# Gated linear recurrence and ELU layer on one core: one activation table set for Ln and Exp, and a remade opening list

## The chip, the cores and the metric

The kernel runs on one core of a Trainium2 chip. The metric is the time of one execution on the device in microseconds, the median of several runs. The core has five engines with queues of their own, each in program order: TensorE (PE, with its weight loads, PEld), VectorE (DVE), ScalarE (ACT), GpSimd (POOL) and SyncE (SP), which here only issues transfers. They wait for each other by semaphores.

## The reference

```python
mag = np.sqrt(a_re * a_re + a_im * a_im)
scale = np.minimum(mag, 0.999) / (mag + 1e-06)
a_re_n, a_im_n = (a_re * scale, a_im * scale)
for t in range(S):
    ar, ai = (a_re_n[:, :, t, :, None], a_im_n[:, :, t, :, None])
    new_re = ar * S_re - ai * S_im
    new_im = ar * S_im + ai * S_re
    kv = np.einsum('bhd,bhe->bhde', k[:, :, t], v[:, :, t])
    S_re, S_im = (new_re + kv, new_im)
    y[:, :, t] = np.einsum('bhd,bhde->bhe', q[:, :, t], S_re)
x = y.transpose(0, 2, 1, 3).reshape(B * S, H * D)
h = x @ w_in
g = np.where(h > 0.0, h, np.exp(np.minimum(h, 0.0)) - 1.0)
out = g @ w_out
```

B = 4 sequences, H = 8 heads, S = 768 steps, D = 48; x is 3072 x 384, w_in 384 x 2048, w_out 2048 x 384. The weights come as float64, all else as float32.

## The kernel before

**Units.** The work is cut into 12 units (u = 0 to 11) of 128 time steps of two sequences. For each unit the recurrence is turned into products: the decays' logarithms and angles are summed over time by matmuls with triangular constants, q and k are scaled by what comes out, and scores, states and outputs are matmuls. Then follows the two-layer part on the unit's 256 tokens.

**Steps of one unit that the change touches.** `squares` (L709, L710; in unit 0 `squared`, L705, by halves) and `joined` (L716, in unit 0 the matmuls of L720) make the squared magnitude. `logarithms` (L735, L736; unit 0: L731) takes Ln, `powers` (L746, L747; unit 0: L742) Exp of multiples of it, `lengths` (L772; unit 0: L766) and `ratios` (L757, L759, L760) and `slopes` (L780) combine these on VectorE. `angles` (L815; unit 0: L811) is an arctan, `carried` (L826) adds the last unit's turn to it. `decays` sums the lengths on TensorE (L889; L932 in unit 1; `sums` L872 and `summed` L879 in unit 0) and takes Exp of the sums (L904, L920). `turned` (L837 on TensorE, L842 to L849 on VectorE) sums the angles to z, `waves` (L973 to L977) takes sine and cosine of z. `scaled` (L982, L986, L992) and `gated` (L1003) put them on q and k; `transposed` (L1023, L1024), `scores` (L1031, L1036; `scored` L1136, L1145), `states` (L1064, L1077 to L1081) and `values` (L1100, L1109, copies L1121 to L1126; later L1177, L1180) follow, and `seam` (L1190) moves the last heads' rows by DMA. `noted` (L791; later L796, L799) checks that the inputs lie in the range in which this way is exact, by the constant `LEAST_RE`; were they not, a slower general path would run after it. `ends` takes the decay at the end of each half (L946 to L954).

**The two layers.** For units 0 to 2 `inner` (L1210) makes two blocks of 128 hidden columns in one PSUM tile `mlp`, of which there are three; `elu` (L1219, L1220 on ScalarE, L1221 on VectorE) empties it; `project` (L1235) multiplies by w_out in four parts of four blocks, with sums in the banks y0 and y1 or, for unit 0, in two of the `mlp` tiles. From unit 3 on (first layer) and unit 2 on (second layer) the products are done with fewer multiplications: `mult` (L1455), `product` (L1319) and sums on VectorE (`summed_in` L1403, L1405; `combined` L1278; `folded` L1297; L1471, L1480).

**Weights.** `fetch` loads a part (L644) as float64; there are eight parts of w_in and eight of w_out. Each call of `convert` puts one of the five VectorE instructions of a part's rounding to float32 in place (L40, L43, L46, L50, L655), so that they lie between other work. `warm` (L1557) is a filler: matmuls of the identity.

**What sets the order.** The scheduler is off (`manual_schedule`). The order in which the functions are called is the order on every engine: first the list `first`, written out by hand, for the opening (to about unit 3), and then a plan in which every step has a place by number (`put`), 16 places to a unit. A step that is in the list is left out of the plan. `table` (L1200) asks for an activation table set at its place; where the set in force lacks a function, a load is put before that function by itself, and is seen under its line.

Of the kernel before, what the change touches and what calls it, by code (L numbers as in the profile page):

```python
# [17 lines left out]
L = 64  # L18
CAP = 0.999
EPS = 1e-6  # L20
LEAST_RE = 0.7
MAGIC = 1.5 * 2.0**23
TURN = 6.2831850

# [481 lines left out]
def kernel(  # L506
# [12 lines left out]
    nc = tc.nc  # L519
# [489 lines left out]
    PAIRED = 2  # L1009
# [496 lines left out]
    def pronounced():  # L1506
# [6 lines left out]


    load_a(0)
    nc.scalar.preload_act_table_set("natural_log")
    ident = const(C, C, "ident")
    nc.gpsimd.memset(ident, 0.0)
    nc.gpsimd.affine_select(
        out=ident, in_=ident, pattern=[[-1, C]], base=0, channel_multiplier=1,  # L1520
# [57 lines left out]
    def gates_of(u, *at):  # L1578
# [5 lines left out]
    first = [  # L1584
        (warm, 1), (warm, 12), (fetch, "in", 0), (begun, 0), (inverses, 0), (inverses, 1),
        (load_qk, 0), (squared, "ar", 0), (load_v, 0), (squared, "ar", 1), (squared, "ai", 0),
        (joined, 0, 0), (squared, "ai", 1), (joined, 0, 1), (logarithms, 0, 0), (logarithms, 0, 1),
        (fetch, "in", 1), (fetch, "in", 2), (ratios, 0, 0), (lengths, 0, 0), (warm, 2), (warm, 1),
        (lengths, 0, 1), (sums, 1), *2 * [(convert,)], (table, "exp_and_others"), (ratios, 0, 1),
        (powers, 0, 0), (powers, 0, 1), (warm, 2), (sums, 0), (warm, 1), (angles, 0, 0),  # L1590
        (angles, 0, 1), (summed, 0), (summed, 1), (decayed, 0, 0), (turned, 0, 0), (decayed, 0, 1),
        (turned, 0, 1), (waves, 0, 0), (waves, 0, 1), (begun, 1), (scaled, 0, "q", 0), (warm, 1),
        (scaled, 0, "k", 1), (scaled, 0, "k", 0), (ends, 0), (scaled, 0, "q", 1), (warm, 1),
        (noted, 0), (convert,), (gated, 0, 0), (warm, 1), (warm, 2), (gated, 0, 1), (warm, 2),
        (convert,), (transposed, 0, "q", 0), (convert,), (transposed, 0, "k", 0),
        (table, "natural_log"), (carry_on, 0), (transposed, 0, "q", 1), (scores, 0, 0),
        *3 * [(convert,)], (load_a, 1), (transposed, 0, "k", 1), (states, 0, 0), (scores, 0, 1),
        (squares, 1), (joined, 1), (fetch, "in", 3), (convert,), (values, 0, 0), (logarithms, 1),
        (powers, 1), (convert,), (states, 0, 1), (warm, 2), (load_qk, 1), (convert,), (lengths, 1),
        (values, 0, 1), (ratios, 1), (seam, 0), (warm, 2), (decays, 1), (load_a, 2), (warm, 1),  # L1600
        (slopes, 1), (convert,), (angles, 1), (convert,), (noted, 1), (convert,), (ends, 1),
        (load_v, 1), (convert,), (turns, 1), (scaled, 1), (inner, 0, 0), (convert,), (inner, 0, 2),
        (fetch, "in", 4), (table, "trig_and_small", 1), (warm, 4), (waves, 1), (gated, 1, 0),
        (convert,), (elu, 0, 0), (convert,), (transposed, 1, "q", 0), (gated, 1, 1),
        (transposed, 1, "k", 0), (load_v, 2), (convert,), (inner, 0, 4), (convert,),
        (fetch, "in", 5), (scores, 1, 0), (states, 1, 0), *2 * [(convert,)],
        (transposed, 1, "k", 1), (convert,), (transposed, 1, "q", 1), (fetch, "in", 6),
        (inner, 0, 6), *2 * [(convert,)], (elu, 0, 2), (convert,), (fetch, "in", 7), (scores, 1, 1),
        (convert,), (values, 1, 0), (states, 1, 1), (values, 1, 1), *3 * [(convert,)], (warm, 2),
        (elu, 0, 4), (seam, 1), (convert,), (inner, 0, 8), *2 * [(convert,)], (inner, 0, 10),  # L1610
        (elu, 0, 8), (convert,), (fetch, "out", 0), (elu, 0, 6), (convert,), (inner, 1, 0),
        (elu, 0, 10), (convert,), (inner, 1, 2), *3 * [(convert,)], (fetch, "out", 1),
        (inner, 1, 4), (fetch, "out", 2), (inner, 0, 12), (fetch, "out", 3), (convert,),
        (inner, 0, 14), (elu, 1, 2), *3 * [(convert,)], (elu, 1, 4), (fetch, "out", 4), (convert,),
        (elu, 1, 0), (convert,), (elu, 0, 12), *2 * [(convert,)], (inner, 1, 6), (convert,),
        (fetch, "out", 5), *2 * [(convert,)], (elu, 0, 14), *3 * [(convert,)], (elu, 1, 6),
        (convert,), (begun, 2), (squares, 2), (convert,), (joined, 2), (convert,), (inner, 1, 8),
        (inner, 1, 10), (convert,), (inner, 1, 12), (fetch, "out", 6), (fetch, "out", 7),
        *2 * [(convert,)], (elu, 1, 8), (convert,), (elu, 1, 10), (convert,), (load_qk, 2),
        *3 * [(convert,)], (elu, 1, 12), *4 * [(convert,)], (project, 1, 0, 0, 4),  # L1620
        (project, 1, 1, 0, 4), (inner, 1, 14), (project, 0, 0, 0, 4), (logarithms, 2), (convert,),
        (powers, 2), (elu, 1, 14), (convert,), (ratios, 2), *2 * [(convert,)], (slopes, 2),
        (convert,), (lengths, 2), (noted, 2), *2 * [(convert,)], (load_a, 3), (angles, 2),
        (carried, 2), (project, 0, 1, 0, 4), (convert,), (project, 0, 0, 4, 8), (convert,),
        (project, 1, 0, 4, 8), *2 * [(convert,)], (project, 1, 1, 4, 8), (decays, 2),
        (table, "trig_and_small", 2), *3 * [(convert,)], (project, 1, 0, 8, 12), *2 * [(convert,)],
        (turns, 2), (project, 0, 1, 4, 8), (begun, 3), *2 * [(convert,)], (waves, 2), (squares, 3),
        (scaled, 2), (ends, 2), (gated, 2), (joined, 3), (project, 1, 1, 8, 12),
        (project, 1, 1, 12, 16), (logarithms, 3), (powers, 3), (states, 2, 0), (load_qk, 3),
        (project, 1, 0, 12, 16), (lengths, 3), (ratios, 3), (project, 0, 0, 8, 12),  # L1630
        (transposed, 2, "k", 0), (transposed, 2, "q", 1), (slopes, 3), (transposed, 2, "q", 0),
        (transposed, 2, "k", 1), (table, "trig_and_small", 3), (angles, 3), (scored, 2), (opened,),
        (carried, 3), (project, 0, 1, 8, 12), (valued, 2), (seam, 2), (noted, 3),
        (project, 0, 0, 12, 16), (summed_in, 0), (summed_in, 1), (combined, 1, 1), (turns, 3),
        (combined, 1, 0), (combined, 2, 0), (waves, 3), (summed_in, 2), (combined, 4, 0),
        (combined, 2, 1), (scaled, 3), (combined, 4, 1), (ends, 3), (load_v, 3), (load_a, 4),
        (project, 0, 1, 12, 16), (gated, 3, None, ('q',)), (inner, 2, 0), (elu, 2, 0),
        (gated, 3, None, ('k',)), (inner, 2, 2), (elu, 2, 2), (inner, 2, 4), (elu, 2, 4),
        (transposed, 3, "q", 0), (summed_in, 3), (inner, 2, 6), (elu, 2, 6), (folded, 2, 0, (3, 1)),
# [135 lines left out]
```

## Time and profile before

| what | us |
|---|---|
| median of three runs (667.33 to 667.91) | 667.35 |
| the profiled execution, its own time | 665.7 |
| its span, first to last instruction | 663.7 |
| PE busy, share of the span | 640.6, 97% |
| VectorE busy, share | 501.9, 76% |
| ScalarE busy, share | 418.9, 63% |
| period of a unit in the middle (L735 at 298.58, 348.92, 399.27) | 50.35 |
| first `inner` matmul of the long run in the opening | 72.21 |
| end of that run, first `project` | 101.23 |

Share of the span means time in which the engine executes an instruction, and in a row of a timeline the first number is the start in us from the span's start and the second the time from the first start to the last end of the instructions that it merges. What stands in square brackets is idle time before it and what ended that. PEclk is the granted share of TensorE's clock; it was 0.99 on average. The program sends 53.58 MB through its main queue, and in the first 25 us the transfers run at 170 GB/s.

### The profile page before, as it was taken

The page shows a single profiled execution, that of the slowest core. Times are in us where ns is not written, and L with a number is a line of the kernel's source. Part 1 is how long each engine was busy: PE and PEld are TensorE (multiplying, and loading weights), DVE is VectorE, ACT ScalarE, POOL GpSimd, SP SyncE. Part 2 cuts the span into 40 slices and gives each one's busy share as a digit, 9 for nine tenths or more (in the row PEclk, how much of TensorE's full clock was granted, in tenths as well). Part 3 has the DMA queues.
Part 4 walks back from the last instruction along what each step waited for, and adds up shares of the span by engine and source line. Part 5 has one row for each costly group of instructions (what it writes and reads, how often), then busy time and mean ns, then how long its engine had stood idle before and what let it go on. Part 6 is the DMA issues. An engine that isn't in the chain of part 4 may idle for free.

```text
span 663.7 us, 17229 instructions
## 1 busy us (share of the span) xinstructions
PE 640.6 (97%) x7236; PEld 580.2 (87%) x7236; DVE 501.9 (76%) x801; ACT 418.9 (63%) x684; POOL 153.8 (23%) x200
## 2 busy tenths in 40 slices
PE   8889999999999899999999999999999999999995
PEld 6868886576897898998998998998998999999995
DVE  5798999967868689578678678678668768764481
ACT  6885367586756566767667667667677677571250
POOL 2000000112124313413403503503503502402000
PEclk9799999999999999999999999999999999999999
DMA  9997745732800713333442442451451551212100
GB/s 164 178 146 117 150 143 155 131 74 48 128 2 16 136 35 85 80 84 80 77 93 72 78 99 62 83 106 50 93 105 46 100 105 44 53 33 61 35 2 30
DMA packets 151443, 56.12 MB, mean 85 GB/s; under 512 B 129684, under 2 KB 143164, under 8 KB 151356
## 3 DMA queue, kind: packets, MB, share of 16 engines
q1 hardware_dynamic: 147616, 53.58, 39.8%
q0 software_dynamic: 3520, 1.20, 1.6%
q8 instruction: 59, 0.97, 0.6%
q14 instruction: 28, 0.23, 0.1%
q10 hardware_dynamic: 220, 0.14, 0.1%
HBM read 48.91 MB, written 4.80 MB: 81 GB/s over the span
## 4 chain that ended last, share of the span: by engine, by line
PE 63%; DVE 14%; ACT 10%; issue 5%; DMA 4%; SPq 3%; DVEq 0%; ACTq 0%
PE mlp L1319 20%; PE mlp L1455 10%; PE mlp L1210 7%; PE y L1455 5%; PE w L1023 4%; DVE g L1471 4%; PE mlp L1235 3%; PE y L1235 3%; PE y L1109 3%; DVE g L1480 3%; SPq L598 3%; DMA w<-in_moe_w_in_dram 3%; PE w L1064 2%; PE w L837 2%; ACT ee L1477 2%
## 5 line engine op out<-in xcount | busy, mean ns | idle before, releaser
L1319 PE MATMUL mlp<-w_out,g 128*128 128x192 f32 x640 | 111.8, 328 | 1.0 <-DVE ee L1331 1.0
L1319 PEld LDWEIGHTS mlp<-w_out,g 128*128 128x128 f32 x640 | 104.2, 190 | 4.4 <-DVE ee L1331 1.6
L1081 POOL TENSOR_TENSOR S<-S,T 128x384 f32<-128x384 f32 x36 | 30.2, 839 | 174.0 <-DVE S L1079 174.0
L1210 PE MATMUL mlp<-x,w_in 128*128 128x256 f32 x288 | 65.1, 384 | 0.2
L1210 PEld LDWEIGHTS mlp<-x,w_in 128*128 128x128 f32 x288 | 54.7, 193 | 9.2 <-DVE g L1221 0.7
L1471 DVE TENSOR_TENSOR g<-g,mlp 128x512 f32<-128x512 f32 x45 | 30.6, 681 | 40.1 <-ACT qt L1024 28.6
L1297 DVE TENSOR_TENSOR g<-g 128x512 f32<-128x512 f32 x80 | 54.4, 694 | 5.0 <-PE mlp L1319 3.8
L1455 PE MATMUL mlp<-x,w_in 128*128 128x128 f32 x424 | 56.2, 275 | 0.4 <-DVE o L1344 0.4
L1480 DVE SCALAR_TENSOR_TENSOR g<-ee,g 128x512 f32<-128x512 f32 x63 | 47.5, 754 | 11.1 <-ACT ee L1477 11.0
L1319 PE MATMUL mlp<-w,g 128*128 128x192 f32 x320 | 54.5, 329 | 0.0
L1319 PEld LDWEIGHTS mlp<-w,g 128*128 128x128 f32 x320 | 51.8, 190 | 0.6
L1455 PEld LDWEIGHTS mlp<-x,w_in 128*128 128x128 f32 x424 | 51.6, 192 | 0.7 <-DVE o L1344 0.6
L1190 POOL DMA_DIRECT2D x<-y x62 | 29.9, 489 | 94.8 <-ACT y L1126 43.5
L1476 ACT ACTIVATE ee<-g 128x512 f32<-128x512 f32 x63 | 39.5, 627 | 17.4 <-DVE g L1471 17.0
L1468 ACT COPY g<-mlp 128x512 f32<-128x512 f32 x36 | 21.1, 585 | 43.9 <-PE mlp L1455 43.7
L1477 ACT ACTIVATE ee<-ee 128x512 f32<-128x512 f32 x72 | 45.4, 631 | 2.3
L1024 ACT COPY qt<-w 128x512 f32<-128x512 f32 x48 | 25.8, 591 | 15.6 <-PE w L1023 15.4
L904 ACT ACTIVATE n<-w 64x384 f32<-64x384 f32 (+1 forms) x60 | 28.1, 486 | 8.9 <-PE w L889 8.3
L973 ACT ACTIVATE cs<-n 128x768 f32<-128x768 f32 (+1 forms) x14 | 10.5, 751 | 35.7 <-DVE n L845 35.6
L1455 PE MATMUL mlp<-x,g 128*128 128x128 f32 x224 | 29.7, 275 | 1.2 <-DVE o L1344 1.2
L1079 DVE TENSOR_TENSOR S<-w,S 128x384 f32<-128x384 f32 x38 | 21.0, 553 | 12.2 <-POOL S L1081 10.0
L1455 PE MATMUL y<-x,w_in 128*128 128x128 f32 x216 | 29.0, 277 | 1.2 <-ACT g L1468 1.2
(222 smaller groups left out, 1428.7 us busy)
## 6 DMA issues: line engine op xcount, KB each, us to landing
w<-in_moe_w_out_dram SPq DMA_DIRECT2D x8, 768.0 KB
g<-in_moe_w_in_dram SPq DMA_DIRECT2D x24, 256.0 KB
g<-in_moe_w_out_dram SPq DMA_DIRECT2D x24, 256.0 KB
w<-in_moe_w_in_dram SPq DMA_DIRECT2D x16, 288.0 KB
vn<-in_v_dram SPq DMA_DIRECT2D x24, 192.0 KB
ar<-in_a_re_dram SPq DMA_DIRECT2D x22, 192.0 KB
ai<-in_a_im_dram SPq DMA_DIRECT2D x22, 192.0 KB
q<-in_q_dram SPq DMA_DIRECT2D x22, 192.0 KB
```

The source lines that it names most:

```text
L904: nc.scalar.activation(out=flat(x[key][to, n : n + 1]), in_=t[of], func=AF.Exp, scale=sign)
L1081: eng.tensor_tensor(out=new_s, in0=new_s, in1=wide, op=ALU.mult)
L1190: eng.dma_start(out=x["x"][ds(j * HP + D, G), i], in_=x["y"][ds(j * HP + i * G, G)])
L1210: nc.tensor.matmul(t[:, e], lhsT=w_in[:, i, ts(f + e, C)], rhs=x["x"][:, i], start=(i == 0), stop=(i == NI - 1),)
L1235: nc.tensor.matmul(x["o", n], lhsT=x["g", f // 8][:, f % 8, ts(n, C)], rhs=w_out[:, f], start=(f == 0), stop=(f == NF - 1),)
L1297: nc.vector.tensor_tensor(out=S_of(u, k, h), in0=a, in1=b, op=op)
L1319: nc.tensor.matmul(to, lhsT=a[:, m], rhs=b[:, m], start=(first and h == 0 and m == 0), stop=False, skip_group_check=True,)
L1455: nc.tensor.matmul(x["c" + c][:, ts(m, C)], lhsT=a[:, m], rhs=x["mix"][p], start=(p == BANKS[c][0] and m == 0), stop=False, skip_group_che ...
L1471: nc.vector.tensor_tensor(out=part(u, to), in0=part(u, a), in1=part(u, b), op=op)
L1476: nc.scalar.activation(out=e, in_=part(u, of), func=AF.Relu, scale=-1.0)
L1477: nc.scalar.activation(out=e, in_=e, func=AF.Exp, scale=-1.0)
L1480: nc.vector.scalar_tensor_tensor(out=part(u, to), in0=nat[u]["e", to], scalar=-1.0, in1=part(u, of), op0=ALU.add, op1=ALU.max,)
```

## The change

Four things are changed. The set `natural_log_exp_and_others` takes the place of `natural_log` and of `exp_and_others` wherever the kernel asks for a set. `LEAST_RE` is 0.7072. In unit 0 the half 0's Exp follows its Ln at once, and the decays stand ahead of the angles. And the list `first` is remade throughout: the order of unit 0 and unit 1, the places of loads and of fillers (37 in both, in other places), of the conversions, and of the steps of units 2 and 3; its end reaches a few steps further. The plan for later units keeps its places. The start of the list, to the first `elu`, its middle, and the rest of the diff:

```diff
-LEAST_RE = 0.7
+LEAST_RE = 0.7072
...
-    nc.scalar.preload_act_table_set("natural_log")
+    nc.scalar.preload_act_table_set("natural_log_exp_and_others")
...
-        (joined, 0, 0), (squared, "ai", 1), (joined, 0, 1), (logarithms, 0, 0), (logarithms, 0, 1),
-        (fetch, "in", 1), (fetch, "in", 2), (ratios, 0, 0), (lengths, 0, 0), (warm, 2), (warm, 1),
-        (lengths, 0, 1), (sums, 1), *2 * [(convert,)], (table, "exp_and_others"), (ratios, 0, 1),
-        (powers, 0, 0), (powers, 0, 1), (warm, 2), (sums, 0), (warm, 1), (angles, 0, 0),
-        (angles, 0, 1), (summed, 0), (summed, 1), (decayed, 0, 0), (turned, 0, 0), (decayed, 0, 1),
-        (turned, 0, 1), (waves, 0, 0), (waves, 0, 1), (begun, 1), (scaled, 0, "q", 0), (warm, 1),
-        (scaled, 0, "k", 1), (scaled, 0, "k", 0), (ends, 0), (scaled, 0, "q", 1), (warm, 1),
-        (noted, 0), (convert,), (gated, 0, 0), (warm, 1), (warm, 2), (gated, 0, 1), (warm, 2),
-        (convert,), (transposed, 0, "q", 0), (convert,), (transposed, 0, "k", 0),
-        (table, "natural_log"), (carry_on, 0), (transposed, 0, "q", 1), (scores, 0, 0),
-        *3 * [(convert,)], (load_a, 1), (transposed, 0, "k", 1), (states, 0, 0), (scores, 0, 1),
-        (squares, 1), (joined, 1), (fetch, "in", 3), (convert,), (values, 0, 0), (logarithms, 1),
-        (powers, 1), (convert,), (states, 0, 1), (warm, 2), (load_qk, 1), (convert,), (lengths, 1),
-        (values, 0, 1), (ratios, 1), (seam, 0), (warm, 2), (decays, 1), (load_a, 2), (warm, 1),
-        (slopes, 1), (convert,), (angles, 1), (convert,), (noted, 1), (convert,), (ends, 1),
-        (load_v, 1), (convert,), (turns, 1), (scaled, 1), (inner, 0, 0), (convert,), (inner, 0, 2),
-        (fetch, "in", 4), (table, "trig_and_small", 1), (warm, 4), (waves, 1), (gated, 1, 0),
-        (convert,), (elu, 0, 0), (convert,), (transposed, 1, "q", 0), (gated, 1, 1),
-        (transposed, 1, "k", 0), (load_v, 2), (convert,), (inner, 0, 4), (convert,),
-        (fetch, "in", 5), (scores, 1, 0), (states, 1, 0), *2 * [(convert,)],
-        (transposed, 1, "k", 1), (convert,), (transposed, 1, "q", 1), (fetch, "in", 6),
-        (inner, 0, 6), *2 * [(convert,)], (elu, 0, 2), (convert,), (fetch, "in", 7), (scores, 1, 1),
...
+        (squared, "ai", 1), (joined, 0, 0), (joined, 0, 1), (logarithms, 0, 0), (lengths, 0, 0),
+        (powers, 0, 0), (logarithms, 0, 1), (ratios, 0, 0), (sums, 0), (lengths, 0, 1), (sums, 1),
+        (warm, 2), (ratios, 0, 1), *2 * [(convert,)], (table, "trig_and_small", 0), (load_a, 1),
+        (fetch, "in", 1), (fetch, "in", 2), (angles, 0, 0), (turned, 0, 0), (angles, 0, 1),
+        (turned, 0, 1), (summed, 0), (powers, 0, 1), (decayed, 0, 0), (warm, 1), (summed, 1),
+        (decayed, 0, 1), (convert,), (waves, 0, 0), (waves, 0, 1), (scaled, 0, "k", 0),
+        (scaled, 0, "q", 0), (begun, 1), (table, "natural_log_exp_and_others", 0),
+        (scaled, 0, "k", 1), (scaled, 0, "q", 1), (ends, 0), (warm, 2), (warm, 1), (warm, 1),
+        (gated, 0, 0), (transposed, 0, "q", 0), (warm, 1), (squares, 1), (warm, 1), (gated, 0, 1),
+        (convert,), (transposed, 0, "k", 0), (noted, 0), (convert,), (joined, 1), (states, 0, 0),
+        (scores, 0, 0), *3 * [(convert,)], (load_qk, 1), (transposed, 0, "k", 1), (convert,),
+        (logarithms, 1), (powers, 1), (fetch, "in", 3), (lengths, 1), (states, 0, 1),
+        (transposed, 0, "q", 1), (values, 0, 0), (warm, 2), (ratios, 1), (scores, 0, 1), (convert,),
+        (noted, 1), (decays, 1), (values, 0, 1), (warm, 2), (seam, 0), (slopes, 1), (carry_on, 0),
+        *3 * [(convert,)], (ends, 1), (warm, 2), (warm, 2), (table, "trig_and_small", 1),
+        (convert,), (angles, 1), (warm, 1), (load_v, 1), (scaled, 1), (turns, 1), (waves, 1),
+        (inner, 0, 2), (inner, 0, 0), (fetch, "in", 4), (fetch, "in", 5), (load_a, 2),
+        (table, "natural_log_exp_and_others", 1), (gated, 1, 0), (gated, 1, 1), (convert,),
+        (elu, 0, 2), *2 * [(convert,)], (transposed, 1, "k", 0), (convert,),
+        (transposed, 1, "q", 0), *2 * [(convert,)], (transposed, 1, "q", 1), (scores, 1, 0),
+        (convert,), (states, 1, 0), (inner, 0, 4), *4 * [(convert,)], (transposed, 1, "k", 1),
+        (values, 1, 0), (scores, 1, 1), (fetch, "in", 6), (fetch, "in", 7), (states, 1, 1),
+        (warm, 4), (convert,), (elu, 0, 0), *2 * [(convert,)], (elu, 0, 4), (values, 1, 1),
+        (seam, 1), *2 * [(convert,)], (inner, 0, 8), (inner, 0, 6), (convert,), (elu, 0, 8),
+        *2 * [(convert,)], (inner, 1, 6), (inner, 1, 0), (fetch, "out", 0), (convert,),
...
+        *2 * [(convert,)], (elu, 0, 12), (convert,), (elu, 1, 10), *3 * [(convert,)], (load_qk, 2),
+        (convert,), (fetch, "out", 6), (convert,), (project, 1, 0, 0, 4), (convert,),
+        (inner, 1, 14), (slopes, 2), *4 * [(convert,)], (project, 1, 1, 0, 4),
+        (project, 0, 0, 0, 4), (angles, 2), (lengths, 2), (fetch, "out", 7), (convert,),
+        (project, 0, 0, 4, 8), (elu, 1, 14), (project, 0, 1, 0, 4), (decays, 2), *2 * [(convert,)],
+        (project, 1, 0, 4, 8), (carried, 2), (convert,), (table, "trig_and_small", 2), (convert,),
+        (turns, 2), (scaled, 2), (convert,), (table, "natural_log_exp_and_others", 2),
+        (project, 0, 1, 4, 8), (convert,), (begun, 3), (waves, 2), *2 * [(convert,)],
+        (table, "trig_and_small", 3), (project, 0, 1, 8, 12), (project, 1, 1, 4, 8), (squares, 3),
+        (gated, 2), (project, 1, 0, 8, 12), *2 * [(convert,)], (joined, 3), (convert,),
+        (transposed, 2, "k", 1), (transposed, 2, "q", 1), (convert,),
+        (table, "natural_log_exp_and_others", 3), (convert,), (ends, 2), (convert,),
+        (logarithms, 3), (powers, 3), (project, 1, 1, 8, 12), (load_qk, 3), (transposed, 2, "k", 0),
+        (convert,), (ratios, 3), (convert,), (lengths, 3), (project, 1, 0, 12, 16), (slopes, 3),
+        (convert,), (transposed, 2, "q", 0), (project, 1, 1, 12, 16), (angles, 3), (scored, 2),
+        (opened,), (states, 2, 0), (valued, 2), *3 * [(convert,)], (seam, 2),
+        (project, 0, 0, 8, 12), (combined, 1, 1), (noted, 3), (carried, 3), (summed_in, 1),
+        (summed_in, 0), (summed_in, 2), (combined, 1, 0), (project, 0, 1, 12, 16), (combined, 2, 0),
+        (combined, 2, 1), (turns, 3), (combined, 4, 1), (combined, 4, 0), (inner, 2, 4),
+        (inner, 2, 6), (ends, 3), (load_a, 4), (inner, 2, 2), (summed_in, 4), (load_v, 3),
+        (inner, 2, 0), (elu, 2, 4), (scaled, 3), (elu, 2, 6), (summed_in, 3), (elu, 2, 2),
+        (waves, 3), (gated, 3, None, ('k',)), (elu, 2, 0), (project, 0, 0, 12, 16), (inner, 2, 10),
+        (gated, 3, None, ('q',)), (transposed, 3, "k", 0), (warm, 2), (begun, 4),
+        (folded, 2, 0, (3, 1)), (load_v, 4), (inner, 2, 8), (squares, 4), (load_qk, 4),
...
-                put(r + (19.45 if u < PAIRED + 4 else 21.1), table, "exp_and_others", u)
+                put(r + (19.45 if u < PAIRED + 4 else 21.1), table, "natural_log_exp_and_others", u)
```

Counted in the order of instructions as it is built, the ScalarE queue has 36 table loads where it had 53. Units 5 to 11 have two each where they had four.

More of the change, by code (lines that the diff above doesn't have):

```diff
@@ L1604 @@
-        (convert,), (elu, 0, 0), (convert,), (transposed, 1, "q", 0), (gated, 1, 1),
-        (transposed, 1, "k", 0), (load_v, 2), (convert,), (inner, 0, 4), (convert,),
-        (fetch, "in", 5), (scores, 1, 0), (states, 1, 0), *2 * [(convert,)],
-        (transposed, 1, "k", 1), (convert,), (transposed, 1, "q", 1), (fetch, "in", 6),
-        (inner, 0, 6), *2 * [(convert,)], (elu, 0, 2), (convert,), (fetch, "in", 7), (scores, 1, 1),
-        (convert,), (values, 1, 0), (states, 1, 1), (values, 1, 1), *3 * [(convert,)], (warm, 2),
@@ L1610 @@
[L1610 to L1639, printed above, removed]
@@ L1640 @@
-        (transposed, 3, "k", 0), (begun, 4), (squares, 4), (summed_in, 4), (inner, 2, 8),
-        (elu, 2, 8), (transposed, 3, "q", 1), (load_v, 4), (load_qk, 4), (summed_in, 5),
-        (combined, 3, 0), (inner, 2, 10), (summed_in, 6),
+        (squared, "ai", 1), (joined, 0, 0), (joined, 0, 1), (logarithms, 0, 0), (lengths, 0, 0),
+        (powers, 0, 0), (logarithms, 0, 1), (ratios, 0, 0), (sums, 0), (lengths, 0, 1), (sums, 1),
+        (warm, 2), (ratios, 0, 1), *2 * [(convert,)], (table, "trig_and_small", 0), (load_a, 1),
@@ new lines @@
+        (values, 1, 0), (scores, 1, 1), (fetch, "in", 6), (fetch, "in", 7), (states, 1, 1),
+        (warm, 4), (convert,), (elu, 0, 0), *2 * [(convert,)], (elu, 0, 4), (values, 1, 1),
+        (seam, 1), *2 * [(convert,)], (inner, 0, 8), (inner, 0, 6), (convert,), (elu, 0, 8),
+        *2 * [(convert,)], (inner, 1, 6), (inner, 1, 0), (fetch, "out", 0), (convert,),
+        (inner, 1, 2), (elu, 0, 6), (convert,), (inner, 1, 4), (fetch, "out", 1), (fetch, "out", 2),
+        (begun, 2), (squares, 2), (fetch, "out", 3), (joined, 2), (elu, 1, 6), *2 * [(convert,)],
@@ new lines @@
+        (elu, 1, 0), *3 * [(convert,)], (elu, 1, 2), (convert,), (elu, 1, 4), (logarithms, 2),
+        (inner, 1, 12), (load_a, 3), *2 * [(convert,)], (inner, 1, 8), (fetch, "out", 4),
+        (inner, 0, 10), (inner, 0, 14), (elu, 1, 12), (inner, 0, 12), (convert,), (fetch, "out", 5),
+        *3 * [(convert,)], (load_v, 2), (powers, 2), (elu, 1, 8), *2 * [(convert,)], (elu, 0, 10),
+        (convert,), (noted, 2), (ratios, 2), *2 * [(convert,)], (elu, 0, 14), (inner, 1, 10),
+        *2 * [(convert,)], (elu, 0, 12), (convert,), (elu, 1, 10), *3 * [(convert,)], (load_qk, 2),
@@ new lines @@
+        (inner, 2, 6), (ends, 3), (load_a, 4), (inner, 2, 2), (summed_in, 4), (load_v, 3),
[3 more added lines that the diff above has]
+        (folded, 2, 0, (3, 1)), (load_v, 4), (inner, 2, 8), (squares, 4), (load_qk, 4),
+        (transposed, 3, "q", 0), (transposed, 3, "q", 1), (summed_in, 5), (combined, 3, 0),
@@ L1643 @@
+        (summed_in, 6), (elu, 2, 10), (summed_in, 8), (joined, 4), (summed_in, 7), (elu, 2, 8),
+        (combined, 3, 1), (inner, 2, 12), (transposed, 3, "k", 1),
     ]
```

## The prediction

> **What bounds the kernel now.** I read the page first (engine shares, slices), then what the tensor engine waits for, then a timeline of one late unit, then the opening's timeline engine by engine.
>
> ```profile
> PE 640.6 (97%) x7236; PEld 580.2 (87%) x7236; DVE 501.9 (76%) x801; ACT 418.9 (63%) x684; POOL 153.8 (23%) x200
> PE   8889999999999899999999999999999999999995
> ```
>
> PE is busy 97% of the span; what it isn't busy lies in the first three slices (to 50 us), in the fourteenth (216 to 232) and at the end. A change elsewhere pays only where it ends a PE wait, or lets PE's dense stretch begin sooner. ACT (63%) pays nothing by itself. Its table loads are in the groups of ACT:
>
> ```profile
> L1200 ACT ACT_TABLE_LOAD x21 | 26.9, 1283 | 0.5
> L746 ACT ACT_TABLE_LOAD x11 | 14.1, 1283 | 0.2
> L735 ACT ACT_TABLE_LOAD x10 | 12.8, 1283 | 0.2
> ```
>
> With the 11 others these are 53 loads of 1.283 us, 68 us of ACT. Now the waits of PE, and one unit's timeline:
>
> ```profile
> PE w L889 <- DVE n L772: 2.0, 8, 0.2
> ```
>
> ```profile
> 298.58 1.28 ACT L735 ACT_TABLE_LOAD   x1
> ...
> 301.07 2.02 DVE L1297 TENSOR_TENSOR g<-g 128x512 f32<-128x512 f32 x3
> 301.46 1.28 ACT L746 ACT_TABLE_LOAD   x1
> 302.76 0.94 ACT L746 ACTIVATE n<-n,ln_eps 128x768 f32<-128x768 f32 x1
> 303.33 1.02 PEld L1100 LDWEIGHTS y<-a,vn 64*64 64x64 f32 x64 [0.23 <-DVE g L1297]
> 303.33 1.16 PE L1100 MATMUL y<-a,vn 64*64 64x64 f32 x64
> ...
> 303.73 0.96 DVE L772 SCALAR_TENSOR_TENSOR n<-n 128x768 f32<-128x768 f32 x1 [0.64 <-ACT n L746]
> ...
> 304.74 0.21 PEld L889 LDWEIGHTS w<-n,sum_logs 64*64 64x64 f32 x8 [0.38 <-DVE n L772]
> 304.74 0.88 PE L889 MATMUL w<-n,sum_logs 64*64 64x384 f32 x8 [0.24 <-DVE n L772]
> ```
>
> The reader is to see a chain: two loads and three functions on ACT, one VectorE operation, then PE. PE waits at its end, but only 0.24 us of matmul (0.38 of weight load). In the opening PE is idle or on fillers until the long run of `inner`:
>
> ```profile
> 9.81 1.28 ACT L1200 ACT_TABLE_LOAD   x1
> ...
> 12.25 1.28 ACT L811 ACT_TABLE_LOAD   x1
> ...
> 14.50 1.28 ACT L920 ACT_TABLE_LOAD   x1
> ...
> 15.07 0.56 DVE L842 TENSOR_SCALAR n<-w 128x384 f32<-128x384 f32 x1 [1.19 <-PE w L837]
> ...
> 17.45 1.28 ACT L973 ACT_TABLE_LOAD   x1
> ...
> 21.39 0.95 DVE L1003 TENSOR_TENSOR qg<-q,cs 128x768 f32<-128x768 f32 x1
> ```
>
> ```profile
> 72.21 29.18 PE L1210 MATMUL mlp<-x,w_in 128*128 128x256 f32 x132
> 101.23 5.32 PE L1235 MATMUL y<-w_out,g 128*128 128x384 f32 x16
> ```
>
> From 72 us to 214 PE has no wait worth naming, so the opening's gain is how much sooner that run ends.
>
> **What the Trainium skill says.** "ScalarE: Activation LUTs", What ACT_TABLE_LOAD costs, gives 1283 ns and a drain of about 1380 for a switch. The trace agrees with the first and shows no drain: the load at 298.58 ends at 299.86 and the next function starts at 299.87. I price 1.28. The same page, Table sets, says that `natural_log_exp_and_others` holds both functions, so no load stands between Ln and Exp. "ScalarE activation tables: per-element evaluation and per-set limits", The table does not change what the instruction takes (in its first section, What a function is on this engine), says that an instruction costs the same whichever table is read; no run yet shows it here, and I keep the durations.
>
> **Part 1, the set in the late units.** The instruction order as built has 36 loads where 53 were. Unit 4 keeps its pair: the unit 2 Exp before it (L1220) had loaded another set. Units 5 to 11, seven of them, lose both: 14 x 1.283 = 18 us of ACT. On PE's path: without loads L735 starts at 298.58, L746 at 300.18 (0.75 + 0.85 later), ends at 301.1. L772 then starts when the three L1297 end, 303.09 instead of 303.73, and ends at 304.05, before PE finishes L1100 at 304.49. So the wait goes, and what is late next is PE itself. Bounds: 0.24 us (the matmul wait) to 0.42 us (start of the last L1100 matmul to L889); I take 0.30, x 7 = **2.1 us** (1.7 to 2.9). The wait at L837 in each unit (0.25 us, its chain starts at L889) moves along and stays. The other 16 us lie beside PE.
>
> **Part 2, the opening.** A walk of the new order with durations from rows of the old profile (in brackets the old time). Four loads in the first 20 us become three.
> - ACT: L731(0) ends 8.51; Exp(0) needs L766(0), queued behind the two reciprocals (to 9.03), so 9.47 to 10.05; L731(1) to 10.5; trig load to 11.8; two L811 (0.47 apart) to 12.76 (14.48); load to 14.06; Exp(1) to 14.68; four L920 with one wait for L879(1) to 16.8 (17.43); load to 18.1; waves to 20.05 (20.69).
> - DVE: angles sooner, L842 at 12.5 + 0.95 = 13.45 (15.07); two rounds of three, the step L46, four L986, L951, 0.8 for L953, so the first L1003 at 19.8 (21.39): 1.6 sooner.
> - ACT again: load to 21.35, q copies to 23.8, squares of unit 1 to 25.4. These need a(1), now issued ahead of two weight fetches: 3.54 MB in front of and with it, at 170 GB/s (the first 25 us) 20.8, plus 2.0, the lag that this load had before (32.1 against 30.1 for 5.11 MB): 22.8, needed at 24.55. Then k copies to 26.55, `noted` (2.1) to 28.65, k copies of the second half to 30.5, unit 1's Ln and Exp without a load (3.4) to 33.8 (39.3), second q copies to 34.8 (29.4: later), x copies, `noted` to 37.85, L920 (1.64) to 39.5 (43.2), seam issue at 40.65 (40.0), trig load, arctan to 44.3 (45.3), waves to 49.55 (50.85).
> - DVE: in1's conversion ends 39.15 (37.15), in2's four steps run between, z of unit 1 is done at 48.75 (50.2), the four L1003 of unit 1 to 52.3 (57.8); before, two conversion steps and more stood between them. Against that it owes in2's last step, three steps of in3 and one L1221: 0.97 + 2.17 + 0.65 = 3.8. Net DVE is 5.5 - 3.8 = 1.7 sooner.
> - From there DVE is dense: in3 (4.05 a part, 63.60 to 67.65 in the trace) to 57.85, in4 to 64.15, the last mask (L1036) 64.8. PE: L1100 and L1109 of unit 1 end at 66.1, and the run starts, of twelve `inner` (2.59 each) and not eleven: 66.1 + 31.1 = 97.2 against 101.2, **4.0 us** sooner.
> - PSUM gates the run: each `inner` needs the elu of the third before it, and those L1221 stand among conversions on DVE. I get 76.1 for a start at 76.5, 78.5 for 79.1, 83.8 for 84.25: margins of half a microsecond. If each is missed, PE falls back to DVE's 1.7. I take **3.2** (0.5 to 4.5: below DVE's share if a few steps are misread by a microsecond, and half a microsecond above the walk; the fillers are 37 pairs in both).
>
> **Part 3, units 2 and 3.** Loads stay at 11. After decays of unit 2 three loads stand in a row and a fourth follows its waves: 3.85 us lie in the time in which PE and DVE make z (7 us from L889), so they cost nothing; if that were short by all, 2.5. w_out's last part is converted at 134.8 and wanted at 134.6. The `project` of unit 0's first 128 tokens now ends after four `inner` of unit 2, so its accumulator holds one of three PSUM slots: the third `inner` waits for the elu of the first, by my sums 0.2 us. I take **0.4 us** lost (0 to 3). From the fold of unit 2 on, the order on DVE is the old one. The stricter least part and `noted` move no instruction.
>
> **Sum.** 2.1 + 3.2 - 0.4 = 4.9. The profiled execution took 665.7 us (span 663.7 and 2.0 around it), so 660.8; the median of the runs lies 1.65 above it, and 667.35 - 4.9 = **662.5**. About 0.2% (1.3 us) is what a measurement of this kernel can tell from no change.
>
> **Rivals.**
> - VectorE keeps the opening: conversions and L1221 miss the margins, or the head start is handed back in units 2 and 3 before 190 us. For it: DVE is 23.5 of 24 us busy from 101 to 125. Against: PE had slack over w_out there (out1 done at 95.0, used at 101). Part 1 alone is left: 667.35 - 2.1 = 665.2.
> - Slower: ACT runs in order, and k copies, `noted` and everything of unit 0's second half are now queued behind the squares of unit 1, which wait for the load of a(1). From a landing at 24.6 us each microsecond goes through to the run. If packets in flight share the engines so that order of issue counts little, a(1) lands at 32.1 as before: 7.5 late, 7.5 - 4.9 = 2.6, so 670.0. It turns slower at 29.5. Against: the first weight part, third in line, was there at 11.85.
> - The late units give nothing, since something else reaches L889 as late (a PSUM slot, another wait on the vector queue): 667.35 - 2.8 = 664.5. The order shows nothing such.
>
> **Chances.** Forecast 0.58 (its own range 660.5 to 664.2), vector bound 0.19, late units nothing 0.07, slower 0.10; 0.06 for more than 7 us gained. Faster by over 0.2% takes the forecast, the last, the third and two thirds of the vector case: 0.81; 0.10 within; 0.09 slower. The range, 660.0 to 666.6, leaves the slower case and the upper end of the vector case out.
>
> **What would show it.** Right: 36 loads; no `L889 <- L772` wait of 0.24 in units 5 to 11 and a period of 50.05 us, not 50.35; first L1003 near 19.8; twelve `inner` without a break from about 66 to 97. Wrong: an idle ACT ahead of L710 that ends with a DMA; PE waiting for L1221 within the run; waits for `mlp` slots between 150 and 185.

## The result and the profile after

The kernel after takes 659.59 us, the median of 20 runs (657.83 to 667.55); the kernel before, run beside it, 667.21 us (20 runs, 665.35 to 668.75). The ratio is 0.989, 95% interval 0.988 to 0.991, so 7.2 us gained (6.1 to 8.3). The forecast was 662.5 with a range of 660.0 to 666.6: the sign and both places of the gain were right, and the gain, put at 4.9 us, came out larger. The median itself lies 0.4 us below that range; the ratio on the 667.35 that the forecast starts from makes 660.1, just inside it. That is past the forecast case's own range (660.5 to 664.2), and 7.2 falls in the case of more than 7 us, which had a chance of 0.06; its interval reaches back into the forecast case. In the profiled executions the span went from 663.7 to 657.0 us.

The shares of the engines and TensorE's slices, from the page of the kernel after:

```profile
PE 637.2 (97%) x7236; PEld 579.7 (88%) x7236; DVE 502.9 (77%) x801; ACT 396.8 (60%) x667; POOL 155.0 (24%) x200
PE   8899999999999899999999999999999999999995
```

ScalarE lost 22 us of work (418.9 before) and 17 instructions, TensorE kept its work, and the third slice is fuller. The groups of table loads that answer to those shown of before:

```profile
L1200 ACT ACT_TABLE_LOAD x24 | 30.8, 1283 | 2.6 <-issue 2.1
...
L735 ACT ACT_TABLE_LOAD x1 | 1.3, 1283 | 0.0
L746 ACT ACT_TABLE_LOAD x1 | 1.3, 1283 | 0.0
```

With the ten others they are 36 loads, where 53 were. Now the waits of TensorE (us in all, times, longest), a late unit, the opening's first gated q, the first steps that need the moved load, and the long run, all of the kernel after:

```profile
PE w L889 <- DVE n L772: 0.2, 1, 0.2
```

```profile
295.82 0.94 ACT L746 ACTIVATE n<-n,ln_eps 128x768 f32<-128x768 f32 x1
...
296.82 2.02 DVE L1297 TENSOR_TENSOR g<-g 128x512 f32<-128x512 f32 x3
298.76 0.95 DVE L772 SCALAR_TENSOR_TENSOR n<-n 128x768 f32<-128x768 f32 x1
299.09 1.02 PEld L1100 LDWEIGHTS y<-a,vn 64*64 64x64 f32 x64 [0.23 <-DVE g L1297]
299.09 1.16 PE L1100 MATMUL y<-a,vn 64*64 64x64 f32 x64
...
300.07 0.83 PE L889 MATMUL w<-n,sum_logs 64*64 64x384 f32 x8
```

```profile
19.82 0.95 DVE L1003 TENSOR_TENSOR qg<-q,cs 128x768 f32<-128x768 f32 x1
...
23.34 0.85 ACT L709 ACTIVATE n<-w 128x768 f32<-128x768 f32 x1
24.08 0.84 ACT L710 ACTIVATE n<-w 128x768 f32<-128x768 f32 x1
```

```profile
65.74 31.56 PE L1210 MATMUL mlp<-x,w_in 128*128 128x256 f32 x144
97.14 2.74 PE L1235 MATMUL y<-w_out,g 128*128 128x384 f32 x8
```

The eight waits at L889 became one (unit 4's). L746 ends at 296.76, 2.1 us before the three L1297 do. L772 has no bracket now: it follows the L1297 at once, and L889 follows L1100 at once. L709 and L710 have no wait for a transfer. The run holds 144 matmuls (12 blocks of 12) in one row, and `project` begins at 97.14 instead of 101.23.

The lead of 6.6 us is read off the start of L889 in successive units (us from each span's start), in one execution of each kernel:

| unit | before | after | lead | lead added |
|---|---|---|---|---|
| first `project` | 101.23 | 97.14 | 4.09 | 4.09 |
| 4 | 199.59 | 195.77 | 3.82 | -0.27 |
| 5 | 254.39 | 250.19 | 4.20 | 0.38 |
| 6 | 304.74 | 300.07 | 4.67 | 0.47 |
| 8 | 405.43 | 399.84 | 5.59 | 0.92 (two units) |
| 9 | 455.77 | 450.06 | 5.71 | 0.12 |
| 11 | 556.07 | 549.43 | 6.64 | 0.93 (two units) |

The period is 49.88 us where it was 50.35. One unit hands 0.34 us back, in a wait of L1064 for L1079 (0.41 us at 441.3) that the old trace lacks in that unit.

### The profile page after: what moved, and what is told of

It reads as the page before. It is cut to its first block, busy times and chain, and to the rows that moved or that the text cites. A ratio compares the mean times of both kernels' runs of the same rounds, so it can differ in the third digit from the quotient of the medians.

```text
span 657.0 us, 17210 instructions
## 1 busy us (share of the span) xinstructions
PE 637.2 (97%) x7236; PEld 579.7 (88%) x7236; DVE 502.9 (77%) x801; ACT 396.8 (60%) x667; POOL 155.0 (24%) x200
## 4 chain that ended last, share of the span: by engine, by line
PE 51%; DVE 9%; ACT 5%; issue 2%; DMA 0%; ACTq 0%; DVEq 0%
PE mlp L1319 24%; PE mlp L1455 10%; PE y L1455 5%; DVE g L1471 4%; PE w L1023 3%; DVE g L1480 3%; PE y L1109 2%; ACT ee L1477 2%; ACT ee L1476 2%; PE w L1064 2%; PE w L837 2%; DVE g L1297 1%; PE y L1100 1%; PE w L889 1%; PE y L1136 1%
## 5 line engine op out<-in xcount | busy, mean ns | idle before, releaser
L1210 PE MATMUL mlp<-x,w_in 128*128 128x256 f32 x288 | 64.1, 380 | 0.0
L1210 PEld LDWEIGHTS mlp<-x,w_in 128*128 128x128 f32 x288 | 54.2, 190 | 8.5 <-issue 0.4
L1297 DVE TENSOR_TENSOR g<-g 128x512 f32<-128x512 f32 x80 | 54.4, 694 | 5.0 <-PE mlp L1319 3.8
```

Of the source, the lines that this page charges most:

```text
L1210: nc.tensor.matmul(t[:, e], lhsT=w_in[:, i, ts(f + e, C)], rhs=x["x"][:, i], start=(i == 0), stop=(i == NI - 1),)
L1297: nc.vector.tensor_tensor(out=S_of(u, k, h), in0=a, in1=b, op=op)
```

## The experiments

The theory: two gains that add. The loads taken out of units 5 to 11 shorten each by 0.46 us, and the remade list brings the opening forward. The rivals: one part is all of it; the list's gain hangs on a late load; VectorE sets the opening.

### The set alone

```diff
-    nc.scalar.preload_act_table_set("natural_log")
+    nc.scalar.preload_act_table_set("natural_log_exp_and_others")
...
-        (lengths, 0, 1), (sums, 1), *2 * [(convert,)], (table, "exp_and_others"), (ratios, 0, 1),
+        (lengths, 0, 1), (sums, 1), *2 * [(convert,)], (ratios, 0, 1),
...
-                put(r + (19.45 if u < PAIRED + 4 else 21.1), table, "exp_and_others", u)
+                put(r + (19.45 if u < PAIRED + 4 else 21.1), table, "natural_log_exp_and_others", u)
```

> The kernel before with the shared set put in everywhere (its name in place of the two, the opening's exp load taken out, 37 loads), and the old opening list kept. Theory (the two parts add, each with its own gain): units 5 to 11 lose both loads, 0.46 us each, 3.2 us, and the opening at most 1 us: the run of inner still begins near 72, the span is 663.7 - 3.2 = 660.5 (659.5 to 660.7), the ratio to before about 0.995. Rival (the late units gain only because the new opening hands them another order on the vector queue): the period stays at 50.35 us and the time is that of before. Rival (the set alone is all of it, the remade list gains nothing): span near 657.

Measured: 663.19 us, ratio 0.9945 (0.9930 to 0.9961), so 3.7 us gained; span 660.8. The run of `inner` begins at 71.25 and `project` at 101.32, as before; from unit 5 to 10 the period is 49.88. The expectation's span was 660.5 (659.5 to 660.7). The late units gain by the set alone, 3.1 us up to L889 of unit 11 (556.07 - 552.99), and the opening nothing.

### The list alone

```diff
-                put(r + (19.45 if u < PAIRED + 4 else 21.1), table, "natural_log_exp_and_others", u)
+                put(r + (19.45 if u < PAIRED + 4 else 21.1), table, "exp_and_others", u)
```

> The kernel after with the load of exp_and_others put back into the plan of the late units, so that unit 5 to 11's logarithms and powers have their two loads again (50 loads); the new opening is kept. Theory (the parts add): the run of inner begins at 65.7 and ends near 97.1 as after, the period of a late unit is 50.35 us again, and the span is 657.0 + 7 x 0.46 = 660.2, ratio to before about 0.994. Rival (the late units' gain came with the opening's order): period 49.88 still, span 657.

This kernel keeps the shared set in its opening. Measured: 661.52 us, ratio 0.9933 (0.9910 to 0.9956), 4.5 us gained; the run begins at 64.47 and `project` at 95.79. The period is 50.35 again, and the wait is back, as TensorE's waits and the unit's timeline in this kernel show:

```profile
PE w L889 <- DVE n L772: 2.0, 8, 0.3
```

```profile
298.23 0.96 DVE L772 SCALAR_TENSOR_TENSOR n<-n 128x768 f32<-128x768 f32 x1 [0.64 <-ACT n L746]
...
299.24 0.88 PE L889 MATMUL w<-n,sum_logs 64*64 64x384 f32 x8 [0.25 <-DVE n L772]
```

3.7 and 4.5 make 8.2 us for the two parts, 7.2 together, within their intervals: the gains add, as far as intervals of 1 us and more to each side can show it.

### One load back, and two

```diff
+            if u > PAIRED + 2:
+                put(r + 12.79, table, "natural_log_exp_and_others", u, 1)
+                put(r + 13.19, table, "natural_log_exp_and_others", u, 2)
```

The first kernel has only the first of the two `put` lines.

> The kernel after with one superfluous load of the shared set ahead of the logarithms of units 5 to 11 (43 loads); nothing else on ScalarE's path to L889 is changed. Theory (slack: without loads L772 waits for the three L1297 and not for the logarithm; one load of 1.28 us is hidden and only the second of the old pair was on the path): at most 0.05 us a unit lost, span 657.0 to 657.4. Rival (each load costs half of the 0.46): 0.23 us a unit, 1.6 us, span 658.6.

> The kernel after with two superfluous loads of the shared set, one ahead of the logarithms and one ahead of the powers of units 5 to 11 (50 loads), where the old kernel had its two; the functions and sets they read stay those of after. Theory (what cost time was ScalarE's 2.57 us, not which set is read): period 50.35 us again, span 657.0 + 3.2 = 660.2. Rival (the gain is due to something else than the loads' time): span 657.

Measured: with one, 657.54 us, ratio 0.9876 (0.9857 to 0.9895), period 49.88; with two, 662.55 us, ratio 0.9928 (0.9906 to 0.9949), period 50.29 to 50.32. With one, then with two:

```profile
295.31 2.02 DVE L1297 TENSOR_TENSOR g<-g 128x512 f32<-128x512 f32 x3
295.72 0.94 ACT L746 ACTIVATE n<-n,ln_eps 128x768 f32<-128x768 f32 x1
...
297.25 0.95 DVE L772 SCALAR_TENSOR_TENSOR n<-n 128x768 f32<-128x768 f32 x1
```

```profile
295.13 2.02 DVE L1297 TENSOR_TENSOR g<-g 128x512 f32<-128x512 f32 x3
...
297.79 0.96 DVE L772 SCALAR_TENSOR_TENSOR n<-n 128x768 f32<-128x768 f32 x1 [0.64 <-ACT n L746]
```

The first load is free: L746 starts 0.4 us after L1297 instead of 1.0 ahead of it, and L772 still starts when L1297 ends. The second sets L772, with the same 0.64 us of wait as the old pair. The profiled spans, 655.5 and 657.8, lie below the theories' 657.0 to 657.4 and 660.2, since the opening was quicker in both executions (last section); the period settles it. It is ScalarE's time that cost, not which table is read. On that the Trainium skill ("ScalarE activation tables: per-element evaluation and per-set limits", What a function is on this engine) is borne out: L746 takes 0.94 us and L735 0.84 to 0.87 with the old sets and with the new one.

### The load of unit 1's a behind the weights

```diff
-        (warm, 2), (ratios, 0, 1), *2 * [(convert,)], (table, "trig_and_small", 0), (load_a, 1),
-        (fetch, "in", 1), (fetch, "in", 2), (angles, 0, 0), (turned, 0, 0), (angles, 0, 1),
+        (warm, 2), (ratios, 0, 1), *2 * [(convert,)], (table, "trig_and_small", 0),
+        (fetch, "in", 1), (fetch, "in", 2), (load_a, 1), (angles, 0, 0), (turned, 0, 0), (angles, 0, 1),
```

> The kernel after with the load of unit 1's a issued behind the two weight parts instead of ahead of them, nothing else. The slower rival of the prediction put to the test: if order of issue sets when the data lands, a(1) comes at 30 to 32 us, the scalar queue stands idle ahead of the first squares of unit 1 from 24 to 30-32, the second half of unit 0 and all of unit 1 come 6 to 7.5 us later, and the run of inner begins at 72 to 73: span 663 to 664.5, about that of the kernel before or slower. Other theory (packets share the engines so that the order of issue counts little, or slack further on takes the delay up): under 1 us lost, span 657 to 658.

Measured: 668.88 us, ratio 1.0032 (1.0011 to 1.0053): slower than the kernel before, and 9.3 us behind after. ScalarE, then TensorE, in this kernel:

```profile
29.88 0.84 ACT L709 ACTIVATE n<-w 128x768 f32<-128x768 f32 x1 [6.64 <-DMA w<-in_a_re_dram]
31.49 0.84 ACT L710 ACTIVATE n<-w 128x768 f32<-128x768 f32 x1 [0.77 <-DMA w<-in_a_im_dram]
```

```profile
74.80 31.35 PE L1210 MATMUL mlp<-x,w_in 128*128 128x256 f32 x144
105.98 2.74 PE L1235 MATMUL y<-w_out,g 128*128 128x384 f32 x8
```

L710 begins 7.4 us later than in after (31.49 against 24.08), and the run 9.1 us later. The 1.7 us over 7.4 may be the clock's (last section: 17.1 us at half here, 6.8 in after); no run separates them. The slower rival was a real mechanism, and the order of issue, a few items in a list, decides between 1.1% gained and 0.3% lost. None of the list's other moves was tried alone but the fillers, so how they share its gain stays open.

### More work for VectorE within the run

```diff
+    for _ in range(more):
+        nc.vector.tensor_scalar(
+            out=p, in0=f, scalar1=F32_EXP, scalar2=None, op0=ALU.bitwise_and
+        )
...
-        yield from _rounded(nc, w, f, p)
+        yield from _rounded(nc, w, f, p, 4 * ((kind, m) == ("in", 5)))
```

Lines below the edit are 4 higher in these kernels (L1214 is L1210).

> The kernel after with four more repetitions of the conversion's L46 (0.59 us each, 2.3 us of VectorE) in one part of w_in within the long run, which change no value. Theory (TensorE holds the run and the elu operations have at least 1.17 us of margin to the next inner): the first inner behind it waits 2.3 less its margin, so the run ends 0.9 to 1.2 us later, and the span is 657.7 to 658.2. Rival (VectorE-bound opening: the run ends when VectorE has done its work): 2.3 us later, span 659.3. Rival (margins of half a microsecond as in the prediction): 1.8 us later.

> The 2.3 us of extra VectorE work once more, since in the first look the granted TensorE clock was half for 15 us in all between 40 and 75 us, which put the start of the run of inner at 71.7 and covered the extra work. In a look with the clock full from 24 us on, the run begins near 64.2. Theory (elu margins of 1.2 to 2.0 us): within the run TensorE waits 0.3 to 1.2 us for L1225, in one or two places. Rival (VectorE-bound): 2.3 us. If the clock drops again, the start is late and no wait is seen.

> Eight extra repetitions in the same part of w_in, 4.7 us of VectorE, no value changed. Theory (margins of 1.2 to 2.0 us, and VectorE's idle time further on takes the rest up): TensorE waits 2.7 to 3.5 us within the run, and the span is 2.7 to 3.5 us longer than that of after at the same clock. Rival (VectorE-bound opening): 4.7 us longer. Rival (TensorE alone counts): under 1 us.

Measured: four repetitions, 660.89 us, ratio 0.9899 (0.9877 to 0.9920), against 0.9892 for after: too close to tell. Its profiled execution is hard to read, since the clock put the run's start at 71.65 and was half to 75.40: the run took 33.02 us to `project`, and that half clock alone makes up 1.9. (Between 40 and 76 us it was half for 13.7 us in all, not the 15 of the second expectation.) The second execution began the run at 66.99 and took 31.54 us, where the kernel with one load back takes 31.18 and after 31.40: at most 0.36 us lost out of 2.35 us added. TensorE's longest wait within it is 0.09 us, less than the theory's 0.3 to 1.2. Eight repetitions: 663.25 us, ratio 0.9938 (0.9921 to 0.9956), 3.1 us behind after. TensorE in that one:

```profile
67.16 5.45 PE L1214 MATMUL mlp<-x,w_in 128*128 128x256 f32 x24
75.02 2.83 PE L1214 MATMUL mlp<-x,w_in 128*128 128x256 f32 x12 [2.42 <-issue]
78.03 2.86 PE L1214 MATMUL mlp<-x,w_in 128*128 128x256 f32 x12 [0.18 <-DVE g L1225]
81.09 20.99 PE L1214 MATMUL mlp<-x,w_in 128*128 128x256 f32 x96 [0.20 <-DVE g L1225]
101.91 2.74 PE L1239 MATMUL y<-w_out,g 128*128 128x384 f32 x8
```

The run takes 34.75 us to `project`, 3.57 over 31.18, out of 4.73 added; the theory had 2.7 to 3.5, VectorE as the bound 4.7. The row marked "issue" is a wait for L1225 too: the one ahead of it ends at 74.92. VectorE doesn't set the run; TensorE does, and what VectorE adds is felt only beyond a slack of some 1.2 us (4.73 - 3.57) to 2 us.

### Without fillers, and with more

```diff
-        (warm, 2), (ratios, 0, 1), *2 * [(convert,)], (table, "trig_and_small", 0), (load_a, 1),
+        (ratios, 0, 1), *2 * [(convert,)], (table, "trig_and_small", 0), (load_a, 1),
```

and so for the other thirteen places. The second kernel is unit 4's (next section) with three pairs more:

```diff
-        (noted, 1), (decays, 1), (values, 0, 1), (warm, 2), (seam, 0), (slopes, 1), (carry_on, 0),
+        (noted, 1), (decays, 1), (warm, 3), (values, 0, 1), (warm, 2), (seam, 0), (slopes, 1), (carry_on, 0),
```

> The kernel after without the 24 pairs of filler matmuls in the opening's list (the 13 ahead of the first load stay); fillers write a slot that nothing reads, so nothing that is computed is left out. One theory (they hold up the granted clock): the half-clock spells between 20 and 60 us, 5 to 7 us long in after, grow by 7 us or more, and the run of inner begins 1.5 us later or more. The other (the clock's spells don't follow them, and each pair only takes TensorE's time and a slot): the run begins at the same time or up to 0.7 us sooner.

> The kernel with unit 4's loads gone (unit4), and three more pairs of fillers in TensorE's wait of 1.23 us ahead of the first-half values' second product, near 36.3 us. The runs so far begin the long run of inner at 64.1 to 64.5 where the clock was half for 3.4 us in all between 8 and 80 us, at 65.7 to 67.0 for 6.8 us, at 68.4 for 10.2 us. One theory (that wait leaves the window of activity around 36 to 41 us too empty): the half spell at 40 to 47 us is gone, the run begins at 64.5 or sooner, span near 655, median 1 us or more under that of unit4 (659.41). The other (the spells fall where they fall[...]): same median as unit4 to 0.7 us.

Measured: without fillers 659.68 us, ratio 0.9897 (0.9864 to 0.9930), run from 66.75, the clock half for 13.7 us in all in its one profile; with three more 659.61 us, ratio 0.9890 (0.9872 to 0.9908), run from 66.48, half for 10.2 us. Neither time differs from its neighbour's by what can be told apart. The fillers, remade or not, are not where the gain lies. They do go with the clock: without them the mean granted clock of the seven runs is 0.976 to 0.990 (median 0.986), where after has 0.983 to 0.997 in 20 (median between 0.993 and 0.994). The three runs at 0.976 to 0.981 took 662.9 to 663.5 us, the four at 0.986 to 0.990 657.8 to 659.7, so without fillers the time spreads with the clock. Three pairs more raised it no further (0.988 to 0.992, against 0.989 to 0.996 in the kernel without them).

### Unit 4's loads too

```diff
-        (turns, 2), (scaled, 2), (convert,), (table, "natural_log_exp_and_others", 2),
+        (turns, 2), (scaled, 2), (convert,), 
...
-        (table, "trig_and_small", 3), (project, 0, 1, 8, 12), (project, 1, 1, 4, 8), (squares, 3),
+        (project, 0, 1, 8, 12), (project, 1, 1, 4, 8), (squares, 3),
...
-        (waves, 3), (gated, 3, None, ('k',)), (elu, 2, 0), (project, 0, 0, 12, 16), (inner, 2, 10),
+        (waves, 3), (gated, 3, None, ('k',)), (table, "natural_log_exp_and_others", 4, 1), (elu, 2, 0), (project, 0, 0, 12, 16), (inner, 2, 10),
```

and in the second kernel besides

```diff
-            noting = r + (15.7 if u != PAIRED + 2 else 17.6)
+            noting = r + (15.7 if u != PAIRED + 2 else 19.3)
```

> The kernel after with one load of the shared set placed ahead of unit 2's first elu, so that unit 4's logarithms and powers find the set loaded, and with the two loads in a row of unit 2 and 3 whose set is replaced before it is used taken out (31 loads). Theory: unit 4's wait of 0.24 us at L889 goes, with up to 0.46 us as in the other units, and what unit 2 gave back (0.27 us) may return: span 656.2 to 656.8. Rival (vector-bound between 205 and 230 us, so that nothing is gained there): 657.0.

> As the one before, and besides the step that notes unit 4's decays (1.9 us of VectorE) is moved behind the mix of its layer. Theory: TensorE's wait of 1.23 us near 212 us (L1455 for VectorE's L1344) is for exactly this queue and goes: up to 1.2 us more, span 655.0 to 655.6, faster than both kernels. Rival (the work is only moved: the next wait, 1.25 us near 225, grows by as much): span as of the one before, 656.2 to 656.8.

Measured: 659.41 us, ratio 0.9874 (0.9852 to 0.9897), and 657.33 us, ratio 0.9859 (0.9836 to 0.9882). The intervals overlap each other's and that of after. The traces say more: TensorE's wait at unit 4's L889 is gone. From L889 of unit 3 to that of unit 4 both take 50.63 us, where six kernels with the new list and unit 4's loads take 51.1 to 51.4 and after itself 51.5: 0.5 us or more. (Without fillers it is 50.45 with the loads, and with three pairs more 50.26 without them, so that fillers move this stretch too.) The move of the notes gains nothing, as TensorE's waits from 185 to 262 us show, first in the kernel without it and then with it:

```profile
PE mlp L1455 <- DVE o L1344: 1.7, 2, 1.2
PE y L1455 <- ACT g L1468: 1.4, 1, 1.4
```

```profile
PE mlp L1455 <- DVE o L1344: 2.2, 1, 2.2
PE y L1455 <- ACT g L1468: 1.6, 1, 1.6
```

Two waits became one that is longer than both: the rival. The span of 655.0 is what the theory had named, but it came from a quick opening (`project` at 95.68, against 99.63 in the kernel without the move), and from there to the end the two take 559.3 and 559.0 us. The lower median comes with a mean clock of 0.994 over its five runs, against 0.9925 over the other's six, and 0.0015 of 657 us is 1.0 of the 2.1 us; the rest lies within the intervals. Unit 4's change is worth keeping by its trace; that it beats the kernel after isn't shown by the times.

## Why the prediction was right, and where its sizes were off

**Part 1, late units.** The mechanism held: 36 loads, the wait gone in units 5 to 11, L772 started by the L1297 and no longer by L746. The term of 0.30 us a unit was mis-sized: the chain gave 0.47, and the period fell to 49.88, not 50.05. TensorE from the start of L1100 to the start of L889 took 1.41 us before and takes 0.98 now, so the whole upper bound (0.42) went, and L889's own eight matmuls took 0.88 us and take 0.83. I had priced the printed wait (0.24) and a little more; the rest sat in rows that looked busy, behind a weight load that waited longer (0.38) than the matmul. 2.1 in the sum (1.7 to 2.9) became 3.1 by the set alone, above that range, and 2.8 in after, where one unit handed 0.34 back. Why L1079 is late there is open: of the kernels with the new list that reach unit 9 before 452 us all but one have the wait, and of those there after 453 none; the late load has one of 0.39 us in unit 5 in its place.

**Part 2, opening.** The walk held at the points that it ended on: first L1003 19.8 (19.82), run from 66.1 (65.74), `project` at 97.2 (97.14). It gave 4.0, and 4.09 was measured. (The walk has unit 0's angles ahead of its decays, as the trace shows, L811 at 12.13 and L920 at 15.01; the section on the change has them the other way round.) That it is so close is luck in part. The walk has no term for TensorE's clock, and executions with the same list up to there had `project` anywhere from 95.23 to 99.63 (the kernels with two loads, and with unit 4's), which is 6.0 to 1.6 us sooner than before. What failed without doubt is the reason for the discount to 3.2, "margins of half a microsecond": in the profile after, L1221 of a slot ends 1.17 to 2.99 us before the `inner` that takes it, TensorE has no wait within the run, and the run with 4.73 us more work lost 3.57, not 4.73. How large the opening's gain is on average, the medians tell only roughly: 4.5 us for the list alone (2.9 to 6.0), against 2.8 in the sum for parts 2 and 3.

**Part 3, units 2 and 3.** 0.4 lost was forecast. 0.27 was measured in after, and 0.0, 0.24 and 0.08 in the list alone and with one load and two, which share the list; no wait for an `mlp` slot of the size feared appears.

**The sum.** 2.8 + 4.09 - 0.27 = 6.6 in the traces, against 4.9; 1.7 of the difference is 0.7 from part 1, 0.9 from the discount and 0.1 from part 3. The first is in every trace without the loads; the second is of this pair of executions. In the chances, the cases that count as faster add up to 0.84, not 0.81.

**Rivals.** "VectorE keeps the opening" fell with the repetitions; "the late units give nothing" with the set alone. The slower one lived in the variant with the late load: I had 670.0 for a landing at 32.1, and 668.88 was measured with L710 at 31.49. That nearness is luck: 7.4 us late against 7.2 gained should have given about the time of before, and 1.7 us more came with the clock or something else. In the change itself L710 ran at 24.08 without a wait.

## What to carry to other kernels

When a wait at the end of a chain is to go, price the distance between the last instruction that was on time and the first that was late, not the printed wait: here it was 0.47 us against 0.24. Ask of each load on such a chain how much of it other work hides: here the first of two was free and the second cost everything. An order of issue is a timing decision for the first in-order engine that reads the data, so ask for each load what stands ahead of it: here moving one behind two weight parts cost 9.3 us.

## What was not expected

The start of the long run varied by 4 us and more among kernels with the same list up to it, and this goes with TensorE's granted clock. The stretch from 8 to 80 us (the last three columns are the clock, the DMA share and GB/s), in the kernel with one load back, in after, and in the first one with four repetitions:

```profile
8.00:80.00 72.00, 67.50 (x823) 56.63 (x822) 67.38 (x104) 49.98 (x94) 3.86 (x7) 0.98 0.88 152
```

```profile
8.00:80.00 72.00, 67.53 (x816) 56.82 (x815) 66.16 (x102) 49.61 (x93) 3.85 (x7) 0.95 0.93 152
```

```profile
8.00:80.00 72.00, 64.77 (x781) 53.65 (x780) 62.38 (x98) 44.78 (x85) 3.78 (x7) 0.88 0.88 141
```

Their runs begin at 64.23, 65.74 and 71.65. Finer, in after:

```profile
40.00:42.00 2.00, 1.63 (x28) 1.54 (x26) 1.32 (x3) 0.33 (x1) 1.79 (x3) 0.86 0.15 34
42.00:44.00 2.00, 2.00 (x10) 1.97 (x10) 1.86 (x4) 1.79 (x2) 0.00 (x0) 0.50 0.09 21
44.00:46.00 2.00, 2.00 (x8) 1.35 (x8) 1.49 (x3) 0.00 (x0) 0.00 (x0) 0.79 0.89 169
```

The clock is halved, and the lost shares, 0.14 + 0.50 + 0.21 = 0.85 of 2 us, are 1.7 us or 3.4 us at half. In every profile here the half-clock time in this stretch is a multiple of 3.4. With the new list it is once where the run starts at 64.05 to 64.49, twice at 65.74 and 66.99, three times at 66.48 to 68.44, four times at 66.75 (without fillers) and five times at 71.65 and 74.80: more of it goes with a later start, not strictly. The Trainium skill ("TensorE: Matmul & The Clock Gate", What's actually happening) has this: the clock drops to half after an idle window of about 3.4 us and comes back after a busy one, and the window runs freely, so where it falls differs between executions. The size and the multiples agree. That idleness sets it is not shown: the first spell, near 20 us, follows 3.4 us in which TensorE was busy for less than 60%, and with the late load TensorE was idle for 6.35 us from 26.5 us and 10.2 us of half clock began at 27.3, but in the 3.41 us before the second spell of after, at 41.45, TensorE was busy for 3.09.

The old list had three such spells in the kernel before and two in the set alone, and `project` at 101.23 and 101.32, so the clock isn't the opening's gain: after, with two, is 4.2 us ahead of the set alone. But it blurs any comparison of two single profiles of this opening by 1.5 us or more. What comes behind the opening hardly moves with it (us, one execution of each; the fourth column is the last less the third):

| kernel | half clock, 8 to 80 us | first `project` | from there to the end | span |
|---|---|---|---|---|
| before | 10.2 | 101.23 | 562.5 | 663.7 |
| the set alone | 6.8 | 101.32 | 559.5 | 660.8 |
| the list alone | 3.4 | 95.79 | 563.0 | 658.8 |
| after | 6.8 | 97.14 | 559.9 | 657.0 |
| one load back | 3.4 | 95.41 | 560.1 | 655.5 |
| two loads back | 3.4 | 95.23 | 562.6 | 657.8 |
| unit 1's a late | 17.1 | 105.98 | 559.8 | 665.8 |
| four repetitions | 17.1 | 104.67 | 559.8 | 664.5 |
| four, second execution | 6.8 | 98.53 | 560.0 | 658.6 |
| eight repetitions | 10.2 | 101.91 | 560.0 | 661.9 |
| without fillers | 13.7 | 97.93 | 559.6 | 657.5 |
| unit 4's loads too | 10.2 | 99.63 | 559.0 | 658.7 |
| the same, notes moved | 3.4 | 95.68 | 559.3 | 655.0 |
| unit 4's, more fillers | 10.2 | 97.67 | 558.8 | 656.4 |

The fourth column follows the loads alone: 562.5 to 563.0 with both in the late units, 559.5 to 560.1 with one or none, 558.8 to 559.3 with unit 4's gone too. The spans that the expectations named were missed by up to 7 us, mostly where the opening differed (664.5 with four repetitions, for 657.7 to 658.2).
